# Attention with a relative bias, then a squared-ReLU layer, on one core: q, k and v as fp32 over SyncE's queue with a GpSimd cast, in place of GpSimd's casting DMAs

## The chip, the core and the metric

The kernel runs on one core of one Trainium2 chip. Times are device microseconds (us) of one execution of the whole program. Lower is better. The kernel before took 379.99 us, the median of three runs (378.57 to 380.06).

## What is computed

There are eight batches of eight heads, 576 positions, 64 numbers to a head. The reference, cut to what matters:

```python
scores = q @ k.transpose(0, 1, 3, 2) / sqrt(64)          # 8 x 8 x 576 x 576
scores = scores + bias_table[bucket(|i - j|)]            # 32 buckets; all distances over 127 share one
attn = softmax(scores)
x = (attn @ v).transpose(0, 2, 1, 3).reshape(4608, 512)  # one row per token
h = maximum(x @ w_in, 0)                                 # 512 -> 2048
out = (h * h) @ w_out                                    # 2048 -> 512, fp32
```

q, k, v and both weights come as fp32 from DRAM. The matmuls run on fp16.

## The kernel before, in words

**Tiling.** The unit of the attention is a pair of heads of one batch: 32 pairs, four to a batch. For a pair, q and k are turned so that the head's 64 numbers lie on the partitions (both heads make 128). TensorE forms the scores (L628, with L652 for the last 64 queries and L677 for the last 64 keys), ScalarE takes the exponent (L639, L662, L687), VectorE multiplies the bands near the diagonal by a table of exponents of the bias (L720), TensorE multiplies by v, which carries a column of ones for the sum (L756, L763), and VectorE divides (L780, L785). The result x is turned once more into the tile xt. The layer behind it works on nine groups of 512 tokens: L1012 is the first product, L1033 or L1035 the ReLU, L1043 the square, L896 and L876 the sums of a Strassen scheme (seven products for eight), L934 the second product, L959 to L966 its reading, L983 the store.

**How q and k come in.** All loads are issued by GpSimd, since its DMAs cast fp32 to fp16 on the way (`loader`, L256 to L266, called with "POOL"). For batches 0 to 3 (`SIX = 4`) `load_six` (L417) fetches six neighbouring rows of a head as one run of 384 numbers to a partition, one DMA for a pair. TensorE turns these in 12 small transposes for each of q and k (L583, 64 by 96), and ScalarE or VectorE copies the result out of PSUM with a stride (L545, L547). From batch 4 on `load_rows` (L430) fetches rows of 64 numbers with three DMAs each for q and k. Of these, SyncE's DMA transposes make qt and kt (L566, `DT_QK = 4`). GpSimd or VectorE copies the corners for the last queries and keys into qz and kz (L610). The staging tiles qs and ks are a ring of five pairs.

**How v comes in.** By whole batches, three buffers: six DMAs of GpSimd for a batch (ten for batch 0), cast on the way, straight into va and vm.

**How x is turned.** For batches 0 and 1 by TensorE (L823, 20 transposes a batch), from batch 2 on (`DT_X = 2`) by SyncE's DMA transposes (L801).

**What sets the order.** Each step is entered in a list with its engine, an assumed duration, what it depends on, its buffers and a due time (`Plan.add`). `Plan.schedule` (L100) places them one after the other: at each turn it takes, over all engines, the step that can start first, and among those of one engine the one that is due first. The program is then written in the order of these assumed starts. So the order on each engine is fixed before the run, whatever the real durations are, and an engine that waits for one step holds up all that stand behind it. The constants at the top (`PERIOD`, `LEAD`, `FAST`, `AHEAD`, `G0`, `GP`) set due times. GpSimd's DMAs use eight semaphores in turn (`r_lane`, L249), so the ninth waits for the first to land. SyncE's and ScalarE's DMAs use eight of their own in the same manner.

Of the kernel before, what the change touches and what calls it, by code (L numbers as in the profile page):

```python
# [10 lines left out]
FP32 = mybir.dt.float32  # L11
# [18 lines left out]
DT_QK = 4  # L30
PERIOD, LEAD, FAST, FASTN = 9800.0, 7200.0, 5100.0, 8
AHEAD, G0, GP = 8700.0, 28800.0, 41600.0
DT_X = 2
RELU_DVE = 3
NSTG, NQK, NPT, NV, NX, NGB, NRT, NY = 5, 4, 2, 3, 5, 2, 3, 4
P_ORDER = "1 2 6 5 3 7 4"
P_LAST = "1 6 2 5 7 3 4"
SIX = 4
ORDER = "q0 i0 q1 i1 k0 v k1 i2 o0 o1 i3 o2 o3"
# [17 lines left out]
class Ring:  # L57
    def __init__(self, n):
        self.free = [(0.0, i) for i in range(n)]


class Buf:


    def __init__(self, ring):
        self.ring, self.left, self.slot, self.until = ring, 0, None, 0.0

# [20 lines left out]
class Plan:  # L88
# [11 lines left out]
    def schedule(self):  # L100
# [12 lines left out]
        while len(done) < len(self.ops):  # L113
# [24 lines left out]
            for b in op.bufs:  # L138
                if b.slot is None:
                    t, b.slot = min(b.ring.free)  # L140
                    b.ring.free.remove((t, b.slot))
                b.left -= 1
                b.until = max(b.until, op.end + LAT[e])
                if not b.left:
                    b.ring.free.append((b.until, b.slot))
# [14 lines left out]
    def _buf_time(op):  # L160
        t, taken = 0.0, {}
        for b in op.bufs:
            if b.slot is None:
                i = taken[b.ring] = taken.get(b.ring, -1) + 1
                if len(b.ring.free) <= i:
                    return float("inf")
# [17 lines left out]
def kernel(  # L184
# [48 lines left out]
    vas = [sb(f"va{i}", [128, 4, H, VW]) for i in range(NV)]  # L233
    v4s = [sb(f"vm{i}", [128, 4, 2, VW]) for i in range(NV)]
# [15 lines left out]
    r_stg, r_qk, r_pt, r_v, r_x = Ring(NSTG), Ring(NQK), Ring(NPT), Ring(NV), Ring(NX)  # L250
    r_gb, r_rt, r_y, r_r = Ring(NGB), Ring(NRT), Ring(NY), Ring(2)
    r_s = {i: Ring(1) for i in (2, 3, 4)}
# [20 lines left out]
    def const(f):  # L273
        return lambda: f
# [96 lines left out]
    for i in range(NSTG):  # L371
        for w in range(2):
            first.append(
                P.add(
                    {"DVE": 90.0},
                    lambda i=i, w=w: io(nc.vector.memset(stg[i][w][96:128, 512:640].bitcast(FP32), 0.0)),
                    due=40 + i,
                )
            )
    v_fix = []  # L380
    for i in range(NV):
        v_fix.append(
            [
                P.add({"DVE": 110.0}, lambda i=i: io(nc.vector.memset(vas[i][:, :, :, 64:66], VSC)), due=30 + i),
                P.add({"DVE": 350.0}, lambda i=i: io(nc.vector.memset(v4s[i].bitcast(FP32), 0.0)), due=30 + i),
            ]
        )
        for e in range(2):
            v_fix[i].append(
                P.add(  # L390
                    {"DVE": 90.0},
                    lambda i=i, e=e: io(nc.vector.memset(v4s[i][ds(64 * e, 64), :, e, 64:66], VSC)),
# [8 lines left out]
    b_v = [Buf(r_v) for _ in range(B)]  # L401
# [27 lines left out]

    def load_rows(p, w):  # L430
# [3 lines left out]
        l_qk[p, w] = [  # L434
            load(
                "POOL", nc.gpsimd,
                lambda e=e: rows(stg[b_stg[p].slot][w])[:, 0:4, ds(64 * e, D)],
                const(src[e, 0:512, :].rearrange("(t p) d -> p t d", p=128)),
                512 * 34.5, first, [b_stg[p]], pdue(),
            )  # L440
            for e in range(2)
        ] + [
            load(
                "POOL", nc.gpsimd,
                lambda: stg[b_stg[p].slot][w][0:64, 512:640].rearrange("p (e d) -> p e d", e=2),
                const(src[:, 512:S, :].rearrange("e p d -> p e d")),
                128 * 34.5, first, [b_stg[p]], pdue(),
            )
        ]

    def load_v_head(b, h):
        l = load(
            "POOL", nc.gpsimd,
            lambda: vas[b_v[b].slot][:, :, h, 0:64],
            const(v[b, h, 0:512, :].rearrange("(t p) d -> p t d", p=128)),
            512 * 34.5, v_all, [b_v[b]], pdue(),
        )
        l_v.setdefault((b, h // 2), []).append(l)

    def load_v_tail(b):  # L460
        for e in range(2):
            l = load(
                "POOL", nc.gpsimd,
                lambda e=e: v4s[b_v[b].slot][ds(64 * e, 64), :, e, 0:64],
                const(v[b, e::2, 512:576, :].transpose([1, 0, 2])),
                256 * 34.5, v_all, [b_v[b]], pdue(),
            )
            for hp in range(4):
                l_v.setdefault((b, hp), []).append(l)

    def load_v(b):
        for tt in range(4):
            l = load(
                "POOL", nc.gpsimd,
                lambda tt=tt: vas[b_v[b].slot][:, tt, :, 0:64],
                const(v[b, :, ts(tt, 128), :].transpose([1, 0, 2])),
                1024 * 34.5, v_all, [b_v[b]], pdue(),
            )
            for hp in range(4):
                l_v.setdefault((b, hp), []).append(l)  # L480
        load_v_tail(b)

    v_all = v_fix[0] + v_fix[1] + v_fix[2]
# [22 lines left out]
    for hp in range(4):  # L506
        for w in range(2):
            load_six(hp, w)
        if hp == 1:
            load_v_tail(0)  # L510
        if hp >= 1:
            for h in range(2 * hp - 2, 2 * hp):
                load_v_head(0, h)
    for h in range(6, 8):
        load_v_head(0, h)
# [591 lines left out]
```

The softmax here doesn't subtract the row's maximum and nothing guards it: scores larger than these inputs give would overflow.

## Time and profile before

The profiled execution took 379.08 us. Its span, from the first to the last instruction, is 377.1 us.

| | before |
|---|---|
| median of three runs | 379.99 us |
| profiled execution | 379.08 us |
| its span | 377.1 us |
| TensorE (PE) busy | 360.3 us, 96% |
| VectorE (DVE) busy | 270.3 us, 72% |
| ScalarE (ACT) busy | 256.6 us, 68% |
| GpSimd (POOL) busy, DMA issues among it | 170.1 us, 45% |
| clock granted to TensorE | full in all slices |
| GpSimd's DMA queue | 86976 packets, 18.36 MB |
| SyncE's DMA queue | 48576 packets, 18.66 MB |
| first matmul | 5.18 us after the start |
| first matmul of the layer behind the attention (L1012) | 38.95 us |

How to read the profile: an engine's busy time says how long it had instructions in work, not what the end of the run waited for. The view by windows gives the busy time of each engine in a stretch; the chain of waits follows the end of the program back from step to step; a DMA packet is one contiguous run that one of the 16 DMA engines moves. The engine that issues a DMA is free again after the issue, and the data land later.

### The profile page before, as it was taken

Reading aid. Unit: us, or ns where it says so; the run is one execution under the profiler, and the core shown is the slowest. Engines: PE = TensorE matmul, PEld = TensorE weight load, DVE = VectorE, ACT = ScalarE, POOL = GpSimd, SP = SyncE. Lnnn points to the kernel's source line nnn. Section 1 sums busy time; section 2 is a strip of 40 time slices with the busy share of each in tenths; the row PEclk is TensorE's granted clock in tenths of the full one; section 3 lists DMA queues with packets and bytes.
Section 4 is the critical chain, followed back from the end, with each engine's and each line's share of the span. In section 5 each row is a group of like instructions: output and inputs, shape, how many; then the busy total and the mean of one; then the engine's idle time right before and its main releaser. Section 6 shows DMA issues by size and latency. Waiting matters only on the chain.

```text
span 377.1 us, 10222 instructions
## 1 busy us (share of the span) xinstructions
PE 360.3 (96%) x4120; PEld 246.2 (65%) x4120; DVE 270.3 (72%) x628; ACT 256.6 (68%) x366; POOL 170.1 (45%) x298
## 2 busy tenths in 40 slices
PE   2879999999999999999999999999999999999985
PEld 1657456745776766777767665766587776666774
DVE  4799798999779657966597569756865593583652
ACT  2799888888768877877876777877756634353320
POOL 7997462773967676636549593553000000000000
PEclk9999999999999999999999999999999999999999
DMA  7999999794999997996999999998201120010103
GB/s 98 146 176 141 191 203 78 104 136 54 67 141 129 135 113 120 103 128 81 112 157 72 169 97 123 115 104 105 82 21 47 47 75 28 30 56 30 56 34 108
DMA packets 135839, 37.81 MB, mean 100 GB/s; under 512 B 116208, under 2 KB 135792, under 8 KB 135792
## 3 DMA queue, kind: packets, MB, share of 16 engines
q0 software_dynamic: 86976, 18.36, 59.4%
q1 hardware_dynamic: 48576, 18.66, 25.4%
q8 instruction: 32, 0.52, 0.6%
q10 hardware_dynamic: 240, 0.13, 0.2%
q14 instruction: 15, 0.12, 0.1%
HBM read 36.87 MB, written 9.44 MB: 123 GB/s over the span
## 4 chain that ended last, share of the span: by engine, by line
PE 87%; DVE 6%; ACT 3%; DMA 2%; issue 1%; POOL 0%; ACTq 0%; DVEq 0%; POOLq 0%
PE f L1012 34%; PE f L934 28%; PE pv L763 9%; PE st L628 8%; PE pv L756 2%; ACT pt L639 2%; PE st L677 2%; PE st L652 2%; DMA ks<-in_k_dram 2%; PE f L583 1%; DVE pt L720 1%; DVE s L896 1%; PE f L332 1%; DVE x L785 1%; ACT pt L662 0%
## 5 line engine op out<-in xcount | busy, mean ns | idle before, releaser
L1012 PE MATMUL f<-xt,w_in_sb 128*128 128x512 f16 (+4 forms) x704 | 143.0, 341 | 0.1
L639 ACT ACTIVATE pt<-st 128x1024 f16<-128x1024 f32 x128 | 126.1, 1025 | 22.4 <-PE st L628 22.3
L1033 ACT ACTIVATE rt<-f 128x512 f16<-128x512 f32 x136 | 81.3, 598 | 64.8 <-PE f L1012 62.6
L1043 DVE TENSOR_TENSOR g<-rt 128x512 f16<-128x512 f16 x144 | 60.9, 424 | 51.8 <-ACT rt L1033 50.5
L1012 PEld LDWEIGHTS <-w_in_sb 128*128 128x128 f16 x704 | 62.8, 98 | 49.0 <-issue 8.2
L720 DVE TENSOR_TENSOR pt<-pt,tb_sb 128x512 f16<-128x512 f16 (+2 forms) x96 | 58.2, 621 | 9.4 <-ACT pt L639 8.9
L934 PEld LDWEIGHTS <-g 128*128 128x128 f16 x576 | 54.3, 98 | 14.5 <-issue 5.1
L763 PE MATMUL pv<-va,pt 128*128 128x65 f16 x1280 | 54.8, 193 | 0.7 <-DVE pt L720 0.7
L934 PE MATMUL f<-w_out_sb,g 128*128 128x256 f16 x432 | 54.3, 273 | 0.0
L763 PEld LDWEIGHTS <-pt 128*128 128x128 f16 x1280 | 50.3, 97 | 3.6 <-DVE pt L720 0.8
L934 PEld LDWEIGHTS <-s 128*128 128x128 f16 x432 | 40.6, 98 | 12.7 <-issue 3.8
L261 POOL DMA_DIRECT2D qs<-in_q_dram x64 | 44.7, 712 | 4.7 <-PE f L583 3.2
L261 POOL DMA_DIRECT2D ks<-in_k_dram x64 | 44.4, 707 | 2.9 <-DMA w_out_sb<-in_moe_w_out_dram 1.8
L610 POOL COPY qz<-qt 64x64 f16<-64x64 f16 x55 | 18.8, 344 | 56.0 <-DMA qt<-qs 27.7
L628 PE MATMUL st<-qt,kt 64*128 64x512 f16 x256 | 40.5, 387 | 1.8 <-ACT pt L639 0.5
L959 DVE SCALAR_TENSOR_TENSOR y<-f,y 128x512 f32<-128x512 f32 x45 | 31.0, 689 | 14.7 <-PE f L934 14.2
L934 PE MATMUL f<-wt,s 128*128 128x256 f16 x288 | 37.1, 273 | 1.0 <-DVE s L896 1.0
L756 PE MATMUL pv<-vm,pm 128*128 128x130 f16 x160 | 35.4, 221 | 0.5 <-DVE x L785 0.3
L785 DVE TENSOR_TENSOR x<-pv,r 128x384 f16<-128x384 f32 x64 | 31.4, 490 | 2.0
L610 POOL COPY kz<-kt 64x64 f16<-64x64 f16 x51 | 18.1, 356 | 29.8 <-DMA kt<-ks 18.0
L261 POOL DMA_DIRECT2D va<-in_v_dram x36 | 31.0, 882 | 0.2
L896 DVE TENSOR_TENSOR s<-g 128x1024 f16<-128x1024 f16 x36 | 24.8, 688 | 0.2
(61 smaller groups left out, 303.9 us busy)
## 6 DMA issues: line engine op xcount, KB each, us to landing
out_dram<-y SPq DMA_DIRECT2D x36, 256.0 KB, 2.4
va<-in_v_dram POOLq DMA_DIRECT2D x28, 128.0 KB, 5.7
qs<-in_q_dram POOLq DMA_DIRECT2D x16, 144.0 KB, 5.6
ks<-in_k_dram POOLq DMA_DIRECT2D x16, 144.0 KB, 5.3
w_in_sb<-in_moe_w_in_dram POOLq DMA_DIRECT2D x4, 512.0 KB, 8.7
w_out_sb<-in_moe_w_out_dram POOLq DMA_DIRECT2D x4, 512.0 KB, 11.3
qs<-in_q_dram POOLq DMA_DIRECT2D x32, 64.0 KB, 3.7
ks<-in_k_dram POOLq DMA_DIRECT2D x32, 64.0 KB, 3.3
```

The costliest lines, as they stand in the source:

```text
L261: lambda: io(eng.dma_start(out=out_(), in_=in_())),
L610: io(eng.tensor_copy(out=dst[qb.slot][rw, rw], in_=src[qb.slot][rw, 512:576]))
L628: nc.tensor.matmul(sets_ps[st.slot][:, e, :], kt[rw, ts(jt, 128)], qt[rw, 0:512], start=True, stop=True,)
L639: nc.scalar.activation(out=p5(pts[pb.slot])[:, jt, :, 0:512], in_=sets_ps[st.slot], func=EXPF, scale=SCALE)
L720: io(nc.vector.tensor_tensor(out=a, in0=a, in1=t, op=MULT))
L756: nc.tensor.matmul(ps[:, i, :, :], pm[:, c : c + 128], vm[:, hp, :, 0:65], start=True, stop=False)
L763: nc.tensor.matmul(ps[:, i, e, :], pt[:, (2 * jt + e) * S + c : (2 * jt + e) * S + c + 128], va[:, jt, 2 * hp + e, 0:65], start=False, sto ...
L785: nc.vector.tensor_tensor(out=xs[xb.slot][:, qt0 : qt0 + nq, :].rearrange("p t (e d) -> p t e d", e=2), in0=ps[:, :, :, 0:64], in1=rs[rb.s ...
L934: nc.tensor.matmul(g_ps[bank[bk].slot][:, ts(s_, HALF)], left(c, s_), right(c), start=(c == 0 and s_ == 0 and i in (1, 6, 5, 7)), stop=(c ...
L1012: nc.tensor.matmul(g_ps[bank.slot][:, a:z], w_in_sb[:, kk, ts(nt, 128)], xt_sb[:, kk, c : c + z - a], start=(kk == 0), stop=(kk == 3),)
L1033: io(nc.scalar.activation(out=rts[rb.slot], in_=g_ps[bank.slot], func=RELUF))
L1043: nc.vector.tensor_tensor(out=gs[gb1.slot][:, nt, :], in0=rts[rb.slot], in1=rts[rb.slot], op=MULT)
```

## The change

- `DT_QK` goes from 4 to 3: batch 3 too is turned by DMA transposes. `DT_X` goes from 2 to 3: x of batch 2 is turned by TensorE. `SIX` goes from 4 to 1: only batch 0 comes in runs of six rows. Batches 1 and 2 of q and k are turned by TensorE in 5 full tiles each (128 by 128) in place of 12 small ones.
- v of all batches, and q and k from batch 1 on, come as fp32 by DMAs that SyncE issues, into a ring of three fp32 tiles (`fs`), and GpSimd casts them into the tiles that the matmuls or transposes read. A fetch of v of a pair is four DMAs and three casts; a fetch of q or of k of a pair is three DMAs and one cast.
- Before the first fetch SyncE copies 32 bytes of the first k tile into a fp32 tile (`started`). So no fetch goes out before the first k has landed, and the first fetch also waits for this small copy.
- GpSimd issues only the eight loads of q and k of batch 0 and the eight of the weights.
- v is kept by pairs, six buffers in place of three batches. Some rings are now taken in a fixed order. The constants of the planner and two orders of work (`P_ORDER`, `ORDER`) change, and the first product of the layer (L1012) is entered as holding the buffer of its squares.

The diff, cut to its core:

```diff
-DT_QK = 4
-PERIOD, LEAD, FAST, FASTN = 9800.0, 7200.0, 5100.0, 8
-AHEAD, G0, GP = 8700.0, 28800.0, 41600.0
-DT_X = 2
+DT_QK = 3
+PERIOD, LEAD, FAST, FASTN = 9600.0, 10000.0, 4500, 6
+AHEAD, G0, GP = 3200.0, 52800.0, 40700.0
+DT_X = 3
-NSTG, NQK, NPT, NV, NX, NGB, NRT, NY = 5, 4, 2, 3, 5, 2, 3, 4
-P_ORDER = "1 2 6 5 3 7 4"
+NSTG, NQK, NPT, NV, NX, NGB, NRT, NY, NF = 5, 4, 2, 6, 5, 2, 3, 4, 3
+CAST, CAST_V, CAST_T = 900.0, 760.0, 300.0
+P_ORDER = "1 2 6 5 7 3 4"
-SIX = 4
-ORDER = "q0 i0 q1 i1 k0 v k1 i2 o0 o1 i3 o2 o3"
+SIX = 1
+ORDER = "k0 q0 i0 i1 k1 o0 v o1 q1 o2 i2 i3 o3"
...
+    def fetch(dmas, casts, bufs, deps):
+        fb = Buf(r_f)
+        deps0 = started
+        if not started:
+            o = P.add(
+                {"SP": 430.0},
+                lambda: io(
+                    nc.sync.dma_start(
+                        out=fs[fb.slot][0:1, 0:8].bitcast(FP16), in_=stg[b_stg[0].slot][1][0:1, 0:16]
+                    )
+                ),
+                l_qk[0, 1], [fb, b_stg[0]], pdue(),
+            )
+            started.append(P.add({"DMA": 10.0}, None, [o], [fb, b_stg[0]], -1e9))
+        landed = []
+        for dst, src, packets in dmas:
+            o = P.add(
+                {"SP": 430.0}, lambda dst=dst, src=src: io(nc.sync.dma_start(out=dst(fs[fb.slot]), in_=src)),
+                deps0 + f_fix, [fb] + bufs, pdue(),
+            )
+            landed.append(P.add({"DMA": packets * 19.0 / 16}, None, [o], [fb] + bufs, -1e9))
+        return [
+            P.add(
+                {"POOL": ns},
+                lambda out_=out_, in_=in_: io(nc.gpsimd.tensor_copy(out=out_(), in_=in_(fs[fb.slot]))),
+                landed + deps, [fb] + bufs, pool_due[0],
+            )
+            for out_, in_, ns in casts
+        ]
...
-        l_qk[p, w] = [
-            load(
-                "POOL", nc.gpsimd,
-                lambda e=e: rows(stg[b_stg[p].slot][w])[:, 0:4, ds(64 * e, D)],
...
+        l_qk[p, w] = fetch(
+            [
+                (
+                    lambda f, e=e: f[:, 0:512].rearrange("p (t e d) -> p t e d", t=4, e=2)[:, :, e, :],
+                    src[e, 0:512, :].rearrange("(t p) d -> p t d", p=128), 512,
+                )
+                for e in range(2)
+            ] + [
+                (
+                    lambda f: f[0:64, 512:640].rearrange("p (e d) -> p e d", e=2),
+                    src[:, 512:S, :].rearrange("e p d -> p e d"), 128,
+                )
+            ],
+            [(lambda: stg[b_stg[p].slot][w][:, 0:640], lambda f: f, CAST)],
+            [b_stg[p]], [],
         )
...
+    def load_v(p):
+        b, hp = divmod(p, 4)
+        l_v[p] = fetch(
+            [
+                (
+                    lambda f, e=e: f[:, ts(e, 256)].rearrange("p (t d) -> p t d", t=4),
+                    v[b, 2 * hp + e, 0:512, :].rearrange("(t p) d -> p t d", p=128), 512,
+                )
+                for e in range(2)
+            ] + [(lambda f, e=e: f[ds(64 * e, 64), 512:576], v[b, 2 * hp + e, 512:S, :], 64) for e in range(2)],
+            [
...
             for p in range(4 + 2 * int(step[1]), 6 + 2 * int(step[1])):
-                load_six(p, "qk".index(step[0]))
+                (load_six if SIX > 1 else load_rows)(p, "qk".index(step[0]))
...
-                    {"PE": 4 * mm(512)}, f1, xt_ready[g] + [l_win[nt // 4]], [bank], due + i * 2000, 0.0, "f"
+                    {"PE": 4 * mm(512)}, f1, xt_ready[g] + [l_win[nt // 4]], [bank, gb1], due + i * 2000, 0.0, "f"
```

## The prediction, made before the changed kernel was run

> **What bounds the kernel now.** I read the windows first, then the chain of waits, the groups, and the DMA view of a few stretches. TensorE (PE) by windows:
>
> ```profile
> 0.00:8.00 8.00, 0.69 (x12) 0.51 (x12) 4.16 (x43) 2.14 (x3) 6.21 (x13) 1.00 0.57 82
> 8.00:16.00 8.00, 7.32 (x160) 5.13 (x160) 4.52 (x11) 6.96 (x10) 7.63 (x11) 1.00 1.68 157
> 16.00:24.00 8.00, 6.38 (x121) 4.14 (x122) 7.80 (x19) 5.60 (x8) 7.35 (x14) 1.00 1.15 153
> 24.00:32.00 8.00, 6.84 (x136) 4.99 (x132) 7.65 (x20) 7.97 (x10) 6.34 (x13) 1.00 1.69 166
> 32.00:40.00 8.00, 7.37 (x121) 5.11 (x119) 6.24 (x18) 7.13 (x12) 6.89 (x14) 1.00 1.16 150
> 40.00:120.00 80.00, 79.66 (x1009) 49.83 (x1008) 70.30 (x158) 67.79 (x97) 48.74 (x84) 1.00 1.16 124
> 120.00:200.00 80.00, 80.00 (x918) 56.99 (x917) 58.18 (x128) 61.08 (x86) 47.41 (x85) 1.00 1.06 115
> ```
>
> The columns are the stretch, its length, and the busy time of PE, PE's weight loads, VectorE (DVE), ScalarE (ACT) and GpSimd (POOL). From 40 us on PE is never idle (80.00 of 80.00), so there only PE's own work counts. In the first 40 us it is idle for 40 - 28.6 = 11.4 us, and every idle microsecond added there is added to the run, because no work of the layer behind can fill it before x of batch 0 exists. That stage runs at ACT's pace: from 24 to 32 us ACT is busy for 7.97 of 8.00. The chain between 18.4 us and the first layer matmul (L1012, 38.95 us) is mostly exponents (L639, L662, L687).
>
> **What the Trainium skill says.** (1) "DMA: Bandwidth & Descriptors", section "SWDGE vs HWDGE vs iDMA": the DMAs of GpSimd and those of SyncE (SP) feed different queues of the same DMA engines, and an engine goes round-robin between them. The trace agrees, run by run. Around 72 us, loads of 768-byte runs (q0, GpSimd's) meet a store of 1024-byte runs (q1, SP's):
>
> ```profile
> q0 software_dynamic: 178, 0.13, 65.7%
> q1 hardware_dynamic: 186, 0.18, 47.7%
> ```
>
> In 1.25 us 178 packets of one queue and 186 of the other went through: one for one. (2) "SBUF — State Buffer", section "Who interferes with whom": a VectorE instruction with two SBUF inputs and a GpSimd instruction that reads SBUF exclude each other for their whole length. The trace fits on GpSimd's side:
>
> ```profile
> L610 POOL COPY qz<-qt x55: 226/238/1018, 17.5 to 263.0; 64x64 f16<-64x64 f16 x55
> ```
>
> A copy that takes 226 ns at best takes up to 1018. (3) "GPSIMD Engine Reference", section 4.1: with one input GpSimd is about at line rate. No run here shows a cast of 640 columns. An estimate from that page: 640 at 1.2 GHz is 0.53 us, plus some 0.18 us of fixed cost (226 ns less 64 columns), 0.7 us; the cast of v is about 0.6 us and two of 0.25.
>
> **TensorE's work.** These are its rows:
>
> ```profile
> L583 PE MATMUL f<-id_sb,qs 96*64 96x96 f16 x192 | 7.3, 214 | 5.2 <-DMA qs<-in_q_dram 5.2
> L583 PE MATMUL f<-id_sb,ks 96*64 96x96 f16 x192 | 7.2, 213 | 2.2 <-DMA ks<-in_k_dram 2.1
> L823 PE MATMUL f<-id_sb,x 128*128 128x128 f16 x40 | 3.3, 219 | 0.5 <-DVE x L785 0.3
> ```
>
> Removed: 12 pairs x 2 x 12 = 288 small transposes. In the chain a block of 24 takes 0.65 us, or 0.325 per tensor, with the change of tile shape up to 0.365: 24 x 0.325 to 0.365 = 7.8 to 8.8 us. Added: batches 1 and 2, 16 tensors x 5 = 80 full transposes. Twelve of L823 hold PE from 35.94 to 36.70, 63 ns each: 5.0 us. x of batch 2 adds 20 x 63 ns = 1.3 us. Net gain 1.5 to 2.5 us, and I take 2.0. At 5 x 63 = 315 ns against 325, full tiles by themselves save next to nothing; the gain is batch 3, which leaves PE. The copies out of PSUM get shorter (750 ns on DVE for a strided 576, 422 for a plain 512), which counts only before 40 us; I give it 0 to -1 us.
>
> **The first scores.** In the compiled order two blocks of table matmuls (L332 before) now stand ahead of the first transposes. They need the bias row, which is ready at 8.0 us. Before, q was turned at 5.18 us and k at 8.02. Now both are turned after 8.0 + 2 x 0.5 = 9.1 us, k after ACT has emptied a table bank (0.6 us): first scores about 10.6 us instead of 9.46. Cost 1.1 us, hidden if anything later is later still.
>
> **The loads before 40 us.** This is the step that decides. GpSimd now issues the eight loads of batch 0's q and k and then, with nothing between, all eight weight loads; each waits only for the one eight before it. At 0.65 us each the first weight load is issued at about 6.5 us (before: 16.0), the last by about 13. Weights alone on the DMA engines look like this, from 42 to 49 us:
>
> ```profile
> q0 software_dynamic: 1442, 1.43, 123.6%
> ```
>
> 16 x 7.0 us / 1442 = 78 ns of an engine per packet. The eight loads are 8 x 512 / 16 = 256 packets per engine: 256 x 78 ns = 20.0 us of all 16 engines.
>
> SP's first fetch waits for the first k (landed at 7.98 us), then for the 32-byte copy (1.9 us, as a small load here takes), so its first packets move at about 11.1 us. The old loads of q and k (1536 packets, some 830 gone by 8.75 us, then 250 per us) end at about 11.5, and so the weights start just then. A fetch of v is 2 x 512 + 2 x 64 = 1152 packets, 72 per engine. SP's 256-byte packets alone, from 213.5 to 214 us:
>
> ```profile
> q1 hardware_dynamic: 548, 0.14, 124.9%
> ```
>
> 16 x 0.5 / 548 = 14.6 ns. One fetch alone would need 1.05 us. One for one with the weights it needs 72 x (78 + 14.6) = 6.7 us. SP's order is v of pairs 0, 1, 2, 3, then k of pair 4: 5 x 72 = 360 packets per engine. That is more than the 262 that GpSimd's queue still holds, so all weights go by before k of pair 4 is through: 11.1 + 262 x 0.078 + 360 x 0.0146 = 36.8 us. A microsecond for the landing and 0.7 for the cast give 38.5 us.
>
> On PE's queue the transposes of this k stand between the second and the third score group of pair 2, ahead of the rest of pairs 1 to 3. Before, that place was reached here:
>
> ```profile
> 26.22 0.39 PE L628 MATMUL st<-qt,kt 64*128 64x512 f16 x2 [0.15 <-ACT pm L687]
> ```
>
> From it to L1012 PE took 38.95 - 26.22 = 12.7 us, by ACT's exponents, and the work ahead of L1012 is nearly the same in both kernels. So L1012 would come at 51.2 us. The q of pair 4 adds to it: its fp32 tile is free only when v of pair 3 is cast (about 37.8), then issue, landing and cast end near 42, and its transposes stand some 1.3 us after those of k: 2 us more. L1012 at 53.2, 14 us late. The earlier stall for v of pair 0 (landing 11.1 + 6.7 + 1 = 18.8, cast 19.9, against 16.2 before) lies inside these 14 us, as does the one above.
>
> Bounds: if SP's queue had precedence, the fetches would be through at 11.1 + 5.3 = 16.4 us and the cost is the 1.1 us above; if the casts wait for DVE again and again, the lateness reaches 18 us. I take 14.
>
> **SP's queue in batches 3 to 7.** SP gets 296 load issues. An issue from DRAM took 356 to 442 ns here, so 0.40 to 0.48 with its gap. Per pair: 10 x 0.40 to 0.48 = 4.0 to 4.8 us; two transposes of q and k at 1.20 and their waits (1.43), 2.9; two of x (1.30), 2.6; 1.1 stores, 0.5. That makes 10.0 to 10.8 us against PE's pace: before, the 16 pairs that SP turned had their first transposes at 114.1 and 258.9 us, 9.65 us apart. It is overfull by 0.35 to 1.15 us a pair over 20 pairs, 7 to 23 us. Five pairs loaded in advance make up for 5 x 4.4 = 22 us. I take 0, with 8 us as the upper end, for stores and transposes of x that hold up what stands behind them. GpSimd's casts (56 x 0.7 + 32 x 1.1 = 74 us) replace its DMA issues and are behind nothing but these waits; to DVE they can cost up to 4 us, none if PE's idle time hides it. The last stretch (PE alone after 300 us) is the same work.
>
> **Sum,** against the profiled execution: 379.1 - 2.0 + 14 + 0 = 391 us. The median of the runs is 0.24% higher (379.99); the difference is left out.
>
> **The rivals.** The likeliest is A, as above: 391 (386 to 396), chance 0.58. B, a partial share: SP's queue gets two packets for each of the weights. Then 180 of these go first, k of pair 4 is cast at 11.1 + 14.0 + 5.3 + 1.7 = 32.1 us, 6 us late and 7 with q: 384 us. For it: small and large packets have not been seen together in these sizes; against it: the one-for-one count. Chance 0.14. C, the other side: the fetches pass the weights. From four packets to one on, k of pair 4 is ready at 11.1 + 7.0 + 5.3 + 1.7 = 25.1 us, before PE reaches its place; then only PE's gain, the tables and the shorter copies are left: 379.1 - 2.0 + 1.1 - 1 = 377 us. Chance 0.15. D: A and the full SP queue, 391 + 8 = 399 us, which shows as PE idle after 120 us. Chance 0.13.
>
> **Numbers.** The range 377.5 to 399 leaves out about half of C and half of D. A measurement of this kernel can tell about 0.5% from no change, 378.1 to 381.9 us. Faster is most of C, 0.12; within 0.5% the rest of C and the lower edge of B, 0.05; slower 0.83.
>
> **What would show it.** In the profile after: L1012 first at 51 to 55 us; PE idle before it for 24 to 26 us, named as a wait of the transposes for GpSimd's cast of ks, and of L756 for the cast of v; SP's and GpSimd's packets in equal number from 12 to 36 us; PE's busy time down by 1.5 to 2.5 us; PE without gaps from 60 us on. The prediction is wrong if L1012 starts at 40 us (C), or if PE has gaps in batches 3 to 7 (D).

## The result, and the profile after

| | before | after |
|---|---|---|
| median | 379.59 us (378.57 to 380.06, four runs) | 453.74 us (452.86 to 454.55, four runs) |
| ratio to before, with its 95% interval | | 1.196 (1.192 to 1.200) |
| profiled execution, its span | 379.08 us, 377.1 us | 453.27 us, 451.5 us |
| PE busy | 360.3 us | 376.7 us |
| mean clock granted to PE | 1.00 | 0.928 |
| first layer matmul (L1012, now L1039) | 38.95 us | 58.20 us |

The prediction was 391 us, with 399 as its upper end. The direction was right, and the size was off by 63 us. The lines that answer to those shown of before follow. First the windows of the kernel after (columns as before: PE, PE's weight loads, DVE, ACT, POOL, PE's clock, share of the DMA engines, GB/s):

```profile
16.00:24.00 8.00, 0.80 (x22) 0.47 (x17) 3.14 (x5) 1.65 (x3) 0.16 (x1) 0.63 1.22 196
24.00:32.00 8.00, 2.35 (x29) 1.75 (x28) 1.62 (x6) 1.02 (x1) 1.28 (x4) 0.50 1.22 196
32.00:40.00 8.00, 6.02 (x61) 3.50 (x62) 3.88 (x7) 4.18 (x5) 2.76 (x10) 0.50 1.04 183
40.00:120.00 80.00, 73.23 (x890) 47.01 (x887) 72.31 (x156) 61.13 (x85) 45.58 (x92) 0.99 0.62 137
120.00:200.00 80.00, 64.79 (x657) 41.76 (x654) 53.52 (x107) 46.38 (x64) 30.66 (x63) 0.91 0.65 137
```

There are two holes. From 16 to 32 us PE works 3.15 of 16 us, and the other engines are idle most of the time with it (the busiest, VectorE, works 4.76), so this is a wait for data. And from 120 to 200 us, where before PE was never idle, it works 64.79 of 80 us, at 0.91 of its clock. The second hole goes on: from 120 to 320 us PE is busy for 159.87 of 200 us.

The difference of the spans, 451.5 - 377.1 = 74.4 us, adds up from PE's side. Up to 120 us PE is idle for 29.6 us (before 11.7), 17.9 more. From 120 to 320 us it is idle for 40.1 (before 0). And it is busy for 376.7 - 360.3 = 16.4 us longer, for less work: 37.4 of its 376.7 busy us lie in stretches of half clock. An estimate: at the full clock these 37.4 would be 18.7, and PE's busy time 358.0 us, 2.3 less than before. 17.9 + 40.1 + 16.4 = 74.4. (The last 5.1 us, behind PE's last matmul, are the same in both.)

The start in PE's timeline (start, length, instruction; in brackets the idle time before it and who ended it):

```profile
25.13 0.27 PE L783 MATMUL pv<-vm,pm 128*128 128x130 f16 x1 [7.28 <-POOL vm L462]
33.86 0.66 PE L704 MATMUL st<-qt,kz 128*128 128x288 f16 x2 [6.38 <-POOL kz L637]
46.58 0.45 PE L617 MATMUL f<-id_sb,qs 128*128 128x128 f16 x5 [2.18 <-POOL qs L462]
58.20 1.04 PE L1039 MATMUL f<-xt,w_in_sb 128*128 128x512 f16 x4
```

PE waits for the cast of v of pair 0 until 25.13 us. It then waits for a small copy that stands on GpSimd's queue behind the cast of v of pair 1, and then for q of pair 4. Packets by queue, from 14 to 34 us:

```profile
q0 software_dynamic: 3258, 3.23, 95.5%
q1 hardware_dynamic: 2810, 0.69, 26.6%
```

2810 packets of SP's queue and 3258 of GpSimd's: nearly one for one, as the prediction took it, with 1024-byte packets against 256-byte ones. At this rate the 72 packets that each of the 16 DMA engines moves for a fetch of v take 72 x 16 x 20 / 2810 = 8.2 us, where the prediction had 6.7.

The later hole in PE's waits from 60 to 320 us (total, times, longest):

```profile
PE st L704 <- POOL kz L637: 24.0, 6, 6.0
PE st L655 <- DMA kt<-ks: 13.5, 2, 9.7
```

Both name a DMA transpose of k: the copy kz reads kt, so what is late is what SP issues. (GpSimd waits for SP as well: 44.8 us in all for fetches of v in front of its casts in that stretch.) SP's queue, from 120 to 320 us, the fetches (shortest, median, longest in ns; first and last start):

```profile
L455 SPq DMA_DIRECT2D f<-in_v_dram x68: 405/524/2099, 120.1 to 314.4; - x68
L455 SPq DMA_DIRECT2D f<-in_q_dram x48: 407/538/1797, 122.5 to 304.8; - x48
L455 SPq DMA_DIRECT2D f<-in_k_dram x48: 413/540/1672, 124.4 to 306.7; - x48
```

And a stretch of its timeline:

```profile
212.72 1.83 SPq L455 DMA_DIRECT2D f<-in_q_dram  x3
214.65 1.77 SPq L455 DMA_DIRECT2D f<-in_k_dram  x3
216.46 1.29 SPq L593 DMA_TRANSPOSE qt<-qs  x1
217.85 1.79 SPq L455 DMA_DIRECT2D f<-in_q_dram  x3
219.74 0.54 SPq L1010 DMA_DIRECT2D out_dram<-y  x1
220.37 3.07 SPq L455 DMA_DIRECT2D f<-in_v_dram  x4
```

SP goes from one instruction to the next with a pause of about 0.05 us (from 120 to 320 us only two pauses are longer than 0.06 us, both under 0.4). In every 20 us from 40 to 320 us it is occupied for 17.6 to 18.7 us. (A few instructions are longer and seem to hold a wait for another engine: a transpose of x took up to 2.3 us, 1.2 in the middle. So a small part of that time is not issuing.) An issue of a fetch takes 0.54 us in the middle and 0.59 in the mean of that stretch; ten of them with their pauses take 5.9 to 6.4 us. The pace of a pair shows in SP's transposes of k, first before, then after:

```profile
L566 SPq DMA_TRANSPOSE kt<-ks x16: 1199/1201/2702, 115.5 to 260.3; - x16
L593 SPq DMA_TRANSPOSE kt<-ks x20: 1234/1272/1380, 116.8 to 334.3; - x20
```

From the first (116.8 us, pair 12) to the last (334.3, pair 31) SP takes 11.45 us for a pair, against 9.65 before. 19 x (11.45 - 9.65) = 34 us, most of the 40.1 us for which PE is idle there.

The clock after such a gap, in windows of PE alone (PE busy, clock, DMA share, GB/s):

```profile
172.00:178.00 6.00, 3.14 (x34) 1.00 0.57 126
178.00:182.00 4.00, 0.00 (x0) 0.57 0.53 115
182.00:186.00 4.00, 1.12 (x5) 0.50 0.50 100
186.00:190.00 4.00, 4.00 (x21) 0.65 0.75 177
190.00:194.00 4.00, 4.00 (x63) 1.00 0.68 155
```

PE stops at 175.1 us and starts again at 184.88. The clock is at half from 178.6 to 188.8: here it falls some 3.4 us into the gap and comes back 3.9 us after PE has started.

Last, the rows of the small costs:

```profile
L462 POOL CAST ks<-f 128x640 f16<-128x640 f32 x28 | 22.2, 792 | 25.3 <-DMA f<-in_k_dram 24.9 <-PE pv L790 0.2
L617 PE MATMUL f<-id_sb,ks 128*128 128x128 f16 x40 | 3.6, 220 | 0.7 <-POOL ks L462 0.7
```

A cast of 640 columns takes 722 ns in the middle and 792 in the mean, where the estimate from the Trainium skill ("GPSIMD Engine Reference", section 4.1) gave 0.7 us. GpSimd's idle time before it is for the fetch (24.9 us in all), not for DVE.

### The profile page after: what moved, and what is told of

Read it like the earlier page. It is cut to its first block, busy times and chain, and to the rows that moved or that the text cites. A ratio compares the mean times of both kernels' runs of the same rounds, so it can differ in the third digit from the quotient of the medians.

```text
span 451.5 us, 10284 instructions
## 1 busy us (share of the span) xinstructions
PE 376.7 (83%) x3932; PEld 254.9 (56%) x3932; DVE 286.0 (63%) x633; ACT 252.2 (56%) x355; POOL 133.8 (30%) x286
## 4 chain that ended last, share of the span: by engine, by line
PE 58%; DMA 14%; DVE 14%; SPq 8%; POOL 2%; issue 2%; ACT 2%; POOLq 0%; DVEq 0%
PE f L961 21%; PE f L1039 21%; PE pv L790 5%; SPq L455 5%; DMA kt<-ks 5%; PE st L655 4%; DMA f<-in_v_dram 4%; DVE pt L747 4%; DVE g L1070 2%; DMA f<-in_k_dram 2%; PE pv L783 2%; DVE s L923 1%; PE st L704 1%; DVE x L812 1%; SPq L828 1%
## 5 line engine op out<-in xcount | busy, mean ns | idle before, releaser
L1039 PE MATMUL f<-xt,w_in_sb 128*128 128x512 f16 (+4 forms) x704 | 146.9, 345 | 0.7 <-DMA xt<-x 0.6
L1060 ACT ACTIVATE rt<-f 128x512 f16<-128x512 f32 x127 | 75.8, 598 | 72.6 <-PE f L1039 67.1
L1039 PEld LDWEIGHTS <-w_in_sb 128*128 128x128 f16 x704 | 63.7, 99 | 48.5 <-issue 10.2
L747 DVE TENSOR_TENSOR pt<-pt,tb_sb 128x512 f16<-128x512 f16 (+2 forms) x96 | 66.7, 710 | 16.4 <-ACT pt L666 16.2
L790 PEld LDWEIGHTS <-pt 128*128 128x128 f16 x1280 | 54.3, 101 | 13.8 <-issue 10.5
L790 PE MATMUL pv<-va,pt 128*128 128x65 f16 x1280 | 58.9, 198 | 0.8 <-DVE pt L747 0.8
L462 POOL CAST va<-f 128x512 f16<-128x512 f32 x32 | 23.7, 740 | 71.1 <-DMA f<-in_v_dram 63.0
L704 PE MATMUL st<-qt,kz 128*128 128x288 f16 x64 | 15.1, 323 | 30.4 <-POOL kz L637 30.4
L714 ACT ACTIVATE pm<-st 128x576 f16<-128x576 f32 x32 | 20.9, 652 | 33.8 <-PE st L704 33.5
L462 POOL CAST qs<-f 128x640 f16<-128x640 f32 x28 | 23.9, 852 | 40.7 <-DMA f<-in_q_dram 40.6
L807 DVE RECIPROCAL r<-pv 128x6 f32<-128x6 f32 x64 | 11.8, 185 | 31.8 <-PE pv L790 31.4
L462 POOL CAST ks<-f 128x640 f16<-128x640 f32 x28 | 22.2, 792 | 25.3 <-DMA f<-in_k_dram 24.9
```

The costliest lines, as they stand in the source:

```text
L462: lambda out_=out_, in_=in_: io(nc.gpsimd.tensor_copy(out=out_(), in_=in_(fs[fb.slot]))),
L747: io(nc.vector.tensor_tensor(out=a, in0=a, in1=t, op=MULT))
L790: nc.tensor.matmul(ps[:, i, e, :], pt[:, (2 * jt + e) * S + c : (2 * jt + e) * S + c + 128], va[:, jt, e, 0:65], start=False, stop=(jt == ...
L1039: nc.tensor.matmul(g_ps[bank.slot][:, a:z], w_in_sb[:, kk, ts(nt, 128)], xt_sb[:, kk, c : c + z - a], start=(kk == 0), stop=(kk == 3),)
L1060: io(nc.scalar.activation(out=rts[rb.slot], in_=g_ps[bank.slot], func=RELUF))
```

## The experiments

The theories, as the experiments began. Theory 1: two separate losses, the weight loads in flight at the start and SP's full queue later. Theory 2: one loss, SP's queue of issues, which sets the pace from the first fetch on. Theory 3: the start is late through the 32-byte copy and the tables. Rivals for the later loss: GpSimd's casts, and the order of the plan. Theory 4 came with the results: at the start, too, it is SP's own issue rate. Times are medians, with the ratio to the kernel before and its 95% interval.

### The loss after 120 us

**steady_gp.** Batches 3 to 7 loaded as before the change, the rest left.

```diff
     def load_rows(p, w):
         ...
+        if b >= DT_QK:
+            l_qk[p, w] = [load("POOL", nc.gpsimd, ...), ...]   # three, as in the kernel before
+            return
     def load_v(p):
         ...
+        if b >= DT_QK:
+            l_v[p] = [load("POOL", nc.gpsimd, ...), ...]       # four, by pairs
+            return
```

> The changed kernel, but q, k and v of batches 3 to 7 are loaded as fp16 by GpSimd's casting DMAs, as in the kernel before (v by pairs): 200 load issues leave SP, 200 go to GpSimd, and 20 pairs' casts go. The start is that of the changed kernel. If the loss after 120 us is that of loading through SP and casting (either part), PE has no gap over 1.5 us after 120 us, its clock stays at 1.0 there, and the run takes 398 to 408 us (453.7 less some 50). If the loss after 120 us comes from the order of the plan or from v kept by pairs, the gaps stay and the run is above 440.

Measured: 400.95 us, 1.056 (1.052 to 1.060). PE from 120 to 320 us:

```profile
120.00:320.00 200.00, 199.86 (x2239) 1.00 1.01 109
```

No gap, the full clock. Loading batches 3 to 7 through SP with casts costs 453.74 - 400.95 = 52.8 us of the 74. The constants of the plan and v by pairs, which stayed, do not make this hole by themselves. The plan places its steps anew when loads move, so the order on the engines is not quite the same; before_sp10 below, whose added issues stand outside the plan, doesn't have this weakness.

**v_soft_fp32.** Only the issues of v leave SP; the fp32 tiles, the bytes and the casts stay.

```diff
         for dst, src, packets in dmas:
+            if soft:                     # v of batches 3 to 7
+                landed.append(load("POOL", nc.gpsimd, lambda dst=dst: dst(fs[fb.slot]), const(src), ...))
+                continue
             o = P.add({"SP": 430.0}, ...
```

> The changed kernel, but the fp32 fetches of v of batches 3 to 7 (80 issues) stand on GpSimd's queue instead of SP's; the fp32 tiles, the bytes and all casts stay as in the changed kernel. SP's issue queue as the cause: per pair SP has 6 issues of 0.6 us instead of 10, so 3.6 + 2.9 + 2.6 + 0.5 = 9.6 us against PE's 9.65, the gaps after 120 us shrink to a quarter or less, and the run takes 405 to 420 us. GpSimd's casts as the cause (or their exclusion of DVE): GpSimd has now more to do, the casts are as many, and the run takes 450 us or more.

Measured: 416.63 us, 1.098 (1.094 to 1.102); PE from 120 to 320 us:

```profile
120.00:320.00 200.00, 189.33 (x2073) 0.97 0.71 143
```

80 issues off SP's queue are worth 37.1 us, with every cast still there and more work on GpSimd. The casts are not the cause. A quarter of the idle time is left, since SP still has six fetch issues for a pair.

**before_sp10.** The other way round: the kernel before, with nothing but SP's issues added.

```diff
+    def extra(p, which, part=0):         # pairs of batches 4 to 7, into spare tiles
+        ...
+            io(nc.sync.dma_start(out=f[:, 256 * e : 256 * e + 256]..., in_=src[0:512, :]...))
+            if which == 2 or e:
+                io(nc.sync.dma_start(out=f[64 * e : 64 * e + 64, 512:576], in_=src[512:S, :]))
     ...
-                    lambda w=w, dst=dst: io(nc.sync.dma_start_transpose(...)),
+                    lambda w=w, dst=dst: io(nc.sync.dma_start_transpose(...)) and extra(p, w),
```

> The kernel before, and nothing of the change but SP's issues: with each pair of batches 4 to 7 SP issues ten more loads of the changed kernel's shapes (fp32, 256-byte runs) into three spare tiles that nobody reads; three behind each transpose of q and k, two behind each of x. No casts. SP's queue as the cause of the loss after 120 us: SP has 6.3 us of work a pair now, and 10 x 0.59 more makes 12.2 against PE's 9.65; over 16 pairs 41 us, less some 9 us that the transposes are ahead, plus some half clock after the gaps: 408 to 430 us, with PE waiting for kt. Casts or the order of the plan as the cause: 379 to 384 us.

Measured: 417.66 us, 1.101 (1.098 to 1.105), 38.5 us for 160 issues of loads that nobody reads. SP takes 12.86 us for a pair. PE from 120 to 320 us:

```profile
120.00:320.00 200.00, 171.40 (x1828) 0.93 1.13 146
```

SP's transposes of k, from which the pace of a pair comes:

```profile
L583 SPq DMA_TRANSPOSE kt<-ks x16: 1199/1215/2405, 117.6 to 310.5; - x16
```

This is a hole like that of the changed kernel, with its clock, made by loads on SP's queue alone. The bytes that these loads add are a rival in this run, but v_soft_fp32 keeps all bytes and gains 37.1 us. Some 9 us of SP's time from 120 to 320 us here are nine waits for an earlier one of these loads to land, not issues. With both runs the cause of the later loss, SP's queue, is shown from both sides.

**before_sp4.** The same with four issues a pair in place of ten (`extra` at the transposes of x only).

> As before_sp10, but only the four loads of v are added with each pair of batches 4 to 7 (64 issues, two behind each transpose of x), none of q and k. If SP's queue costs nothing until its work fills PE's pace: 6.3 + 4 x 0.59 = 8.7 us a pair are under 9.65, so 378 to 383 us. If every issue delays what stands behind it (in-order queue, transposes of x held up): four tenths of what ten cost (38 us), so 392 to 396 us.

Measured: 380.01 us, 1.002 (1.000 to 1.004); PE is busy for all 200.00 us from 120 to 320. Each issue takes about as long as in the changed kernel:

```profile
L258 SPq DMA_DIRECT2D f<-in_v_dram x32: 567/576/1614, 156.2 to 309.1; - x32
L264 SPq DMA_DIRECT2D f<-in_v_dram x32: 501/509/1426, 156.9 to 310.6; - x32
```

So 64 issues cost 0.8 us and 160 cost 38.5. The price is not paid by the issue: with four more a pair SP is occupied for some 8.1 us of each pair, under PE's 9.65, and with ten more a pair takes it 12.86. Where between the two the price starts, no run shows more closely.

**before_cast.** The kernel before with the casts alone added, in the same places.

```diff
+    def extra(p, which, part=0):
+        ...
+            io(nc.gpsimd.tensor_copy(out=h, in_=f))            # 128 x 640, for q and for k
+            ...                                                # 128 x 512 and two of 64 x 64 for v
```

> The kernel before, and nothing of the change but the casts: with each pair of batches 4 to 7 GpSimd casts one spare fp32 tile twice in 640 columns, once in 512 and twice in 64 x 64, as the changed kernel does for q, k and v (some 2.6 us a pair); nobody reads the results. SP's queue as the cause of the loss: 379 to 383 us. The casts (GpSimd's queue, or GpSimd and DVE shutting each other out) as a cause: 388 us or more, with PE waiting for DVE or for kz.

Measured: 382.55 us, 1.008 (1.006 to 1.011): 3.3 us for 16 pairs of casts. This includes the fills of the spare tiles at the start, where the first layer's matmul comes 1.3 us later (40.3 us). The forecast of "up to 4 us" was for all 32 pairs with GpSimd's DMA issues gone; here half as many casts come on top of these issues. The run shows that the casts are small against 52.8 us, and doesn't test the 4 us.

### The start

**weights_late** moves the weight issues on GpSimd's queue, nothing else.

```diff
-    for op in P.schedule():
+    ops = [o for o in P.schedule() if o not in w_issue]
+    for n, o in ((2, l_v[3][-1]), (6, l_qk[4, 0][-1])):
+        at = ops.index(o) + 1
+        ops[at:at] = w_issue[:n]
+        del w_issue[:n]
+    for op in ops:
```

> The changed kernel with one thing moved: GpSimd issues the first two weight loads after the cast of v of pair 3 and the other six after the cast of q of pair 4 (in the changed kernel all eight stand ahead of the first cast). Nothing else is moved. Theory 1 (two separate losses: the weights ahead of the fetches delay the first layer by about 19 us, SP's full issue queue costs the rest later): L1045, the first layer's matmul, starts at 40 to 46 us instead of 58.2, and the run takes 434 to 441 us. Theory 2 (one loss: SP's queue of 296 load issues sets the pace from 12 us to 335 us, so a better start is given back later): L1045 is earlier too, but the run gains only what SP's issues lose to the backlog before 60 us, some 10 us: 442 to 447. Theory 3 (the start is late because of the 32-byte copy and the tables, not the weights): L1045 later than 52 us, the run above 448.

Measured: 454.10 us, 1.196 (1.193 to 1.200). The first layer's matmul (L1040 in this kernel; the line number in the expectation is off) starts at 52.9 us, 5.3 us earlier, and the run gains nothing. Theory 1 falls as it stood: the two early weight loads now meet q of pair 4 (SP's issues take up to 2.4 us there), the six later ones meet v and q of batch 1, and PE waits 7.7 us for a cast of q at 69 us instead. What was to come at 40 to 46 us didn't.

**both** is weights_late and steady_gp together.

> weights_late and steady_gp together: the weights issued after the casts of v and q, and batches 3 to 7 loaded by GpSimd as before. Theory 1: the two losses are separate and add: 378 to 388 us, L1045 near 42 us, no gaps after 120 us. Theory 2: as theory 1 here. Theory 3: L1045 later than 52 us and 395 to 405 us.

Measured: 402.66 us, 1.061 (1.058 to 1.064). With the later hole closed, later weights still gain nothing.

**both2** spreads the weights further.

```diff
+    for o, names in ((l_qk[4, 0][-1], "i0"), (l_qk[7, 1][-1], "i1"), (l_v[5][-1], "i2"), (l_qk[7, 0][-1], "i3 o0 o1 o2 o3")):
         ...
+    at = ops.index(l_qk[9, 0][-1]) + 1
+    ops[at:at] = sums
```

> The kernel both, with the weight loads spread: the first behind the cast of q of pair 4, the second behind the cast of k of pair 7, the third behind that of v of pair 5, the fourth and the four of the second layer behind that of q of pair 7, VectorE's sums of the second layer's weights behind the cast of q of pair 9. Theory 1: single weight loads hold a fetch up by 2.5 to 5 us each and the long run of them comes when batch 1 is loaded; 385 to 394 us against 402.7. Theory 4 (SP's issue rate): no gain, 399 to 405.

Measured: 405.47 us, 1.069 (1.062 to 1.075). The first layer starts at 46.4 us, but this line makes the run useless for the question:

```profile
81.45 0.27 PE L821 MATMUL pv<-vm,pm 128*128 128x130 f16 x1 [12.04 <-DVE x L850]
```

VectorE's sums, which I moved too, waited for the last weights in front of the work of x. That is a stall of my own making; the run is inconclusive.

**no_weights** leaves the weight loads out of steady_gp.

```diff
     def load_w_in(u):
-        l_win.append(load("POOL", nc.gpsimd, ...))
+        l_win.append(P.add({"DVE": 600.0}, lambda: io(nc.vector.memset(w_in_sb[:, :, ts(u, 512)], 0.0)), due=900 + u))
```

> The kernel steady_gp (batches 3 to 7 loaded by GpSimd), but no weights are loaded: VectorE fills both weight tiles with zeros instead, so the layers compute zeros; leaves out 8 loads of 512 KB. Theory 1, as the run with later weights changed it (a weight load in flight takes half of the DMA engines' turns from SP's 256-byte packets, wherever it stands, so the fetches of batch 0 and 1 and 20 us of weights get in each other's way): first layer matmul near 40 us, no PE gap over 3 us after 20 us, 379 to 388 us. Theory 4 (SP's own issue rate: 24 issues of 0.6 us stand ahead of q of pair 4 and 56 in all before pair 7): PE still waits for casts of q at 32 and at 50 to 70 us, 390 us or more.

Measured: 396.34 us, 1.045 (1.042 to 1.047), 4.6 us less than steady_gp; the fills delayed the tables by 1.1 us. **no_weights2** moves the fills to where VectorE has time.

> As no_weights (the layers compute zeros, 8 loads of 512 KB are left out, batches 3 to 7 loaded by GpSimd), but VectorE fills the weight tiles between 20 and 28 us (first layer) and after 60 us (second), not in the first 8 us. Weights in flight as the cause of the late start: 380 to 388 us, against 401 with them. SP's own issue rate as the cause: 392 to 397 us, with PE still waiting for casts of q.

Measured: 404.57 us, 1.066 (1.063 to 1.069), 3.6 us more than steady_gp. In its PE timeline:

```profile
49.76 0.71 PE L644 MATMUL f<-id_sb,qs 128*128 128x128 f16 x5 [6.01 <-POOL qs L462]
83.07 2.06 PE L988 MATMUL f<-w_out_sb,g 128*128 128x256 f16 x10 [2.29 <-DVE w_out_sb L562]
```

Without any weight in flight PE still waits 6 us for a cast of q, and the second layer now waits for my late fill. Between -4.6 and +3.6 us, the weights' share in the end time is not told in size; it is not the 13 to 20 us that theory 1 gave it. The fetch queue itself does gain by it: SP has issued the 56 fetches of batches 0 and 1 by 48.6 us in no_weights, and by 65.2 us in steady_gp. But the first layer's matmul comes only 4 us earlier (56.0 for 60.0). SP is occupied for 17.8 of the 20 us from 20 to 40 with no weights in the way (no_weights): its own issues fill it, and q of pair 6 stands behind 16 issues of v.

**no_token** takes the 32-byte copy out of steady_gp, and **start_free** takes out the copy and the weights.

```diff
-        if not started:
-            ...
-            started.append(P.add({"DMA": 10.0}, None, [o], [fb, b_stg[0]], -1e9))
```

> The kernel steady_gp without the 32-byte copy: SP's first fetch waits for nothing but the zeroed tiles and is issued near 4 to 6 us instead of 12.3. Weights as the cause: v of pairs 0 to 2 is through before the weights begin, two fetches are left to share with them: some 12 us less than 401, so 387 to 391 us. SP's issue rate as the cause: SP is at most 7 us ahead: 393 to 397 us. If the fetches now hold up q and k of pair 0: 400 us or more.

> no_weights2 and no_token together: no weights (zeros in their place), no copy to wait for. Either cause: 380 to 390 us; SP's issue rate alone: 385 to 390, since 56 issues of 0.6 us still need until some 40 us.

Measured: no_token 408.43 us, 1.077 (1.075 to 1.079), worse than with the copy, though SP starts at 2.6 us instead of 12.3. The planned order differs with it, and PE waits three times for GpSimd (6.2, 4.4 and 8.9 us). start_free 396.62 us, 1.046 (1.043 to 1.049): nothing stands in SP's way, and the run still takes 17.5 us more than before. Theory 3 falls. start_free came out over 6 us above what either theory gave.

**qk12_sp** has v of all batches loaded by GpSimd, so that SP fetches q and k of batches 1 and 2 only (`if True:` in `load_v` of steady_gp).

> The kernel steady_gp, with v of batches 0 to 2 loaded as fp16 by GpSimd as well, so that SP fetches only q and k of batches 1 and 2: 48 issues instead of 96, and the weights come behind v's loads in GpSimd's queue. If SP's issues make the start late: q of pair 4 is issued near 18 us instead of 27 to 30, and the run lies near all_gp: 390 to 395 us. If not: 398 us or more.

Measured: 397.53 us, 1.050 (1.045 to 1.055), 3.4 us less than steady_gp for half the issues, between the two expectations.

### The parts of the change that don't go through SP

**all_gp.** No fetch by SP, no cast; the change's plan, full tiles and v by pairs stay (`if True:` in both loaders, and fills of the stage tiles as in the kernel before).

> The changed kernel with all q, k and v loaded as fp16 by GpSimd's casting DMAs: nothing is fetched through SP and nothing is cast by GpSimd. The plan, the full tiles of batches 1 and 2, v by pairs and the early weight loads (after the loads of pair 3 in GpSimd's queue, v behind them) stay as the plan orders them. If all the loss comes from SP's fetches and the casts: 376 to 386 us, L1074 (the first layer's matmul) near 40 us. If the plan's order or v by pairs has a part in it: L1074 later than 45 us and more than 388 us.

Measured: 392.36 us, 1.034 (1.032 to 1.037). The first layer (L1086 in this kernel) is nearly on time, at 40.5 us, but PE is idle for 5.5 us from 40 to 60 us, 3.9 of them in one wait for x behind VectorE's sums of activations, and GpSimd is busy for 17 of each 20 us up to 60 us, since a pair has ten DMA issues now where q and k of batch 1 had two. So the new plan with ten issues a pair, all of them on GpSimd, costs 13.2 us. Whether the changed kernel, where SP issues most of them, pays the same, this run doesn't tell.

**before_full** takes only the full tiles of batches 1 and 2 and SP's transposes of batch 3 into the kernel before (`SIX = 1`, `DT_QK = 3`, row loads for all but batch 0). **before_dt3** takes only the latter (`SIX = 3`, `DT_QK = 3`).

> The kernel before, and of the change only that q and k of batches 1 and 2 are turned in full tiles on PE, and those of batch 3 by SP: row loads by GpSimd, three issues for a tensor instead of one (48 issues more), the plan's constants, the order of the loads and v by batches as before. TensorE: 8 tensors at 0.325 us go to SP, 16 change from 325 to 315 ns: 2.8 us less. If the 13 us that all_gp still lost come from the issues on GpSimd's queue in the first 60 us (0.65 to 0.75 us each): 384 to 394 us. If they come from the plan's constants or from v by pairs: 375 to 379 us.

> The kernel before with one thing of the change: batch 3's q and k are loaded by rows and turned by SP's DMA transposes instead of by PE (96 small transposes go, 8 DMA transposes and 16 issues of GpSimd come). Nothing is added before 60 us. TensorE has 2.6 us less, SP has room (6.3 of 9.65 us a pair): 375.5 to 378 us. If SP's queue or the DMA transposes are in the way even here: 379.5 us or more.

Measured: before_full 413.03 us (408.56 to 415.59), 1.085 (1.080 to 1.090); before_dt3 383.34 us, 1.012 (1.009 to 1.014). In before_dt3 PE is busy for 1.5 us less than before (358.7 against 360.3; 2.6 forecast), and the run is 4 us longer. Its profiled execution, the fastest of the six, is 2.2 us longer: from 120 to 320 us PE has small gaps (4.3 us), most of them for ACT's y and for xt. before_full came out far over both expectations. It has 14.6 us of gaps from 160 to 320 us, the longest waits for transposes of x, and what in the old constants makes them was not traced further. No kernel of this study beats the one before.

## Why the prediction was wrong, step by step

The prediction said slower, and slower it was. But most of the loss came from a term that it had set to nothing, so the direction speaks only in part for its working.

The differences between the runs, from the medians (379.2 us is that of before beside all_gp). They add up by construction, and are prices of parts only as far as the parts don't overlap: the plan, full tiles and ten issues a pair on GpSimd, 392.36 - 379.2 = 13.2 us; loading v of batches 0 to 2 and q and k of 1 and 2 through SP with casts instead, 400.95 - 392.36 = 8.6; likewise all of batches 3 to 7, 453.74 - 400.95 = 52.8.

- **The step that failed: "SP's queue in batches 3 to 7 ... I take 0, with 8 us as the upper end".** It is 52.8 us. Three terms were off. An issue was priced at 0.40 to 0.48 us with its gap, from loads that stood alone in the trace of before; one behind the other they take 0.54 in the middle and 0.59 in the mean, and 0.05 between them: ten of them 5.9 to 6.4 us a pair instead of 4.0 to 4.8. So a pair took SP 1.80 us more than PE's pace, where the working had 0.35 to 1.15. "Five pairs loaded in advance make up for 22 us" counted a credit that doesn't exist: loading ahead is itself work of SP's queue, which is full from 40 us on (17.6 to 18.7 of every 20 us). And the gaps brought the half clock, of which the prediction had no word: steady_gp's PE is busy 364.4 us, that of after 376.7, with the same 3932 matmuls: 12.3 us. The other 40.1 are PE's idle time from 120 to 320 us. The threshold itself, PE's 9.65 us a pair, fits: before_sp4 lies below it and loses 0.8 us, before_sp10 lies above it and loses 38.5. The working had put the kernel on the wrong side of it too, and then set the loss to nothing by the credit.
- **Rival D** (the full queue, "PE idle after 120 us") named the mechanism and its sign in the profile. It had 399 us and a chance of 0.13.
- **"The loads before 40 us. This is the step that decides", as a forecast of the place.** It was fair: packets nearly one for one (2810 to 3258), PE idle before the first layer for 26.6 us where 24 to 26 were forecast, 2.2 us of wait for q of pair 4 where 2 were. The first layer came at 58.2 us, where 53.2 was forecast. Most of these 5 us are the clock again, which the working left out: of the 19.3 us by which the first layer is later than before, 15.2 are idle time, and 4.1 are longer busy time, with the clock at half from 18.1 to 42.0 us. The wait that was named, of the transposes for the cast of ks, took only 0.7 us. PE's two long waits, 7.3 and 6.4 us, are both for fetches of v: for the cast of v of pair 0, which was named, and for a copy into kz that stands behind the cast of v of pair 1. The price of SP's packets alone, 14.6 ns, was read from a stretch in which they are those of a transpose of x; beside the weights a fetch of v took 8.2 us instead of 6.7.
- **The same step, as the one that decides.** That was wrong: the larger loss lies behind 120 us. How much of the rest the weights make is not settled. Moving them away gains nothing, leaving them out changes 4 us in either direction. With them SP needs 53 us for the 56 fetch issues of batches 0 and 1 (12.4 to 65.2 us, steady_gp), and without them still 36 (12.5 to 48.6, no_weights). So two causes lie over each other, and with one away the other still holds PE up. What share each has stays open, since later fills, moved sums and a changed order each disturbed a run.
- **First scores** at 10.6 us: 10.68. **Casts**: 0.72 us for 0.7. Their cost to DVE, "up to 4 us", was not measured as such; 16 pairs of them cost 3.3 us in before_cast.
- **TensorE's own work**, 2.0 us less: the estimate of 2.3 us above, with the half clock taken out, agrees. In the measured busy time the slower clock covers it. before_dt3 shows a part of it (1.5 us where 2.6 were expected). A detail: that PE is never idle from 40 us on is right for the line from 120 to 200 us; from 40 to 120 us the prediction's own line has 79.66 of 80.00, on which nothing rests.
- **Not in the working of the start:** that row loads and v by pairs make ten DMA issues of a pair. Batches 0 to 3 had two for q and k of a pair, and v had six to ten for four pairs. The working counts the packets of the first fetches, and prices their issues only for batches 3 to 7. all_gp, with these issues on GpSimd, takes 13.2 us more than the kernel before. How much of that is the issues and how much the plan's constants is open, and so is what of it the changed kernel pays.

The Trainium skill, "DMA: Bandwidth & Descriptors", section "Issuing engines are not separate DMA queues", says that spreading DMAs over engines only saves the sequencer's time to initiate them, which "is usually small relative to the DMA itself". For these loads the measurement decides otherwise: a load of 512 runs needs, by an estimate from the 14.6 ns of the prediction's line (packets of 256 bytes too), 512 x 14.6 / 16 = 0.47 us of the DMA engines, and its issue takes 0.54 us of SP. v_soft_fp32, which only moves 80 issues to another queue, gained 37 us. "TensorE: Matmul & The Clock Gate", section "Part 1: The HAM clock gate", says that PE's clock is at half after an idle window of about 3.4 us, until about 3.4 us of work have passed. The trace of the changed kernel agrees roughly: in its six gaps after 120 us the half clock began 2.6 to 4.4 us into the gap and ended 3.4 to 6.1 us after it. The first gap, at 17.9 us, doesn't fit (last section).

## What to carry to other kernels

Count an engine that only issues DMAs as an engine: its issues for one round, priced back to back, against the round of the engine that bounds the kernel. Below that pace more issues cost next to nothing (64 more: 0.8 us); above it the kernel takes the queue's pace (12.86 us a pair instead of 9.65 in before_sp10), and the gaps cost TensorE's clock on top. When two waits end close to each other, taking one away proves little; take each away alone and both together before one is called the cause.

## What the runs showed of the hardware that was not expected

- A load that SP issued right behind another took 0.58 us of its queue in the middle for 512 runs of 256 bytes, and 0.51 for 64 runs (before_sp4). After a pause of over 0.3 us four loads of steady_gp took 0.37 to 0.38. While the weights of GpSimd's queue were in flight, a single issue took up to 3.2 us.
- In steady_gp 200 issues moved from SP to GpSimd, which takes longer for each (0.53 to 0.83 us, 0.76 in the middle), and with the casts gone the run was 53 us shorter: which queue is full counted here, not the price of an issue.
- Each of the eight gaps of PE of 3.7 us or more in the changed kernel was met with half the clock, and no other stretch of its span was; before there was none. But the length of a gap is not the rule: in the first, at 17.9 us, the half clock began 0.3 us into it, when PE had worked 2.1 of the 3.4 us before. In before_full three stretches of half clock followed gaps of at most 2.2 us, and in before_cast one began at 23.4 us with no gap over 0.7 us before it, PE having worked 2.4 of the last 3.4 us. All these stretches last 3.4 us or a multiple of it (6.8, 10.2, 23.9).
